# Order of loads and weight preparation in the opening of an mLSTM and MLP kernel

## The chip, the core and the metric

The kernel runs on one core of a Trainium2 chip. The metric is the device time of one execution in microseconds. TensorE is called PE here, VectorE DVE, ScalarE ACT, GpSimd POOL and the engine that issues most DMAs SP, as in the profile.

## The reference

The reference has two parts. The first is a recurrence over 768 positions, for 4 batches of 8 heads with head size 40. The second is a multilayer perceptron on its output, 3072 tokens by 320, with a hidden width of 2048:

```
m_new = max(f + m, i);  fs = exp(f + m - m_new);  is = exp(i - m_new)
C = fs * C + is * outer(v, k);   n = fs * n + is * k
y = sigmoid(o) * (C @ q) / max(|n . q|, 1)
x = y as tokens by 320;   h = x @ w_in;   out = (h * sigmoid(h)) @ w_out
```

The inputs are float32, but w_in and w_out arrive as 64-bit floats.

## The kernel before

**Units.** The recurrence is done in chunks of 128 positions. A unit is one chunk of one batch with all 8 heads, so there are 24 units, and units 0 to 3 are the first chunk of the four batches. For each unit the kernel loads `raw` (q and k, transposed), `D` (the running sum of the log forget gates, spread over all partitions) and `kvo` (k, v and the output gate). Then it goes through these steps:

- `decay` (L346): POOL masks D, ACT takes eight exponentials per unit (L364).
- `scores` (L374): PE multiplies k and q (L393), DVE weighs v (L405) and the scores (L412).
- `values` (L416): PE multiplies scores and v (L432), DVE divides and applies the gate and leaves `x` (L439 to L449).
- `state` (L455): PE makes the new state (L461), DVE masks it into `Cm` (L483).
- `xpose` (L490): PE transposes x (L494 to L497), ACT copies it into `xh` (L501) and DVE writes the rest into `xl` (L502). This feeds the perceptron.

**Steps.** Three units make a step of 384 tokens, eight steps in all. A step needs the x of its three units. It runs over 16 chunks of the hidden width: `mm1` (L517, products at L531) multiplies x with a chunk of w_in, ACT and DVE apply the activation, and `mm2` (L555, products at L571) multiplies the result with a chunk of w_out, two chunks later. Step 0 keeps the activation whole (g, L539), later steps split it in two.

**Weights.** The weights come in 18 parts, in the order c0, i0, o0, i1, o1, i2, o2, i3, o3, c4, i4 and so on. A part i holds rows 0 to 255 of w_in for two chunks of the hidden width, a part c holds rows 256 to 319 for eight chunks, and a part o holds the w_out rows of two chunks. `wload(n)` issues the DMAs of the next n parts (L166; L170 and L171 for c). `wmake(n)` makes the next n parts (L173): ACT takes the absolute value (L183), DVE turns the 64-bit float into a 32-bit one in four instructions (L184, L185, L188, L194), and for a part i or c ACT and DVE split it into two (L204 and L205, or L214 and L215). After each make, `wmake` loads one more part.

**What sets the order.** SP's order is that of the program, by hand. For the other engines a planner orders the instructions when the kernel is built: an earlier place in the program is a higher priority, and what is ready in its own reckoning goes first. DVE's order inside the first call of `gates` is by hand too. `gates(lo, hi)` (L101) works out the gate sums for some positions and writes them to DRAM (L124), where the loads of D read them. Raw tiles, weight parts and the x of a step share a pool of ten buffers (`NBIG`); the gates use four of these at the start. A load waits until a buffer is free.

The opening, L635 to L678, is a list of calls ahead of the loop over the steps. In the loop, `FILL` gives the number of weight parts that are made after each chunk of step 0.

Of the kernel before, what the change touches and what calls it, by code (L numbers as in the profile page):

```python
# [43 lines left out]
def mlstm_mlp_kernel(  # L44
# [56 lines left out]
    def gates(lo, hi):  # L101

        init = NEG if lo == 0 else m_t[:, lo - 1 : lo]
        nc.vector.tensor_tensor_scan(
            m_t[:, lo:hi], f_t[:, lo:hi], i_t[:, lo:hi], init, op0=ALU.add, op1=ALU.max
        )

        l1 = max(lo, 1)
        eng = nc.vector
        eng.tensor_tensor(  # L110
            out=f_t[:, l1:hi], in0=f_t[:, l1:hi], in1=m_t[:, l1 - 1 : hi - 1], op=ALU.add
        )
        eng.tensor_tensor(
            out=f_t[:, l1:hi], in0=f_t[:, l1:hi], in1=m_t[:, l1:hi], op=ALU.subtract
        )
        nc.vector.tensor_scalar(f_t[:, l1:hi], f_t[:, l1:hi], -120.0, None, op0=ALU.max)
        if lo == 0:
            nc.vector.memset(f_t[:, 0:1], 0.0)
        for c in range(lo // L, hi // L):
            sl = slice(c * L, (c + 1) * L)  # L120
            nc.vector.tensor_tensor_scan(
                LF[:, sl], one.broadcast_to([BH, L]), f_t[:, sl], 0.0, op0=ALU.mult, op1=ALU.add
            )
        nc.sync.dma_start(LFd[:, 0:H, lo:hi], LF[:, lo:hi])  # L124
        nc.scalar.dma_start(LFd[:, H, lo:hi], LF[0:B, lo:hi])
        eng.tensor_tensor(
            out=i_t[:, lo:hi], in0=i_t[:, lo:hi], in1=m_t[:, lo:hi], op=ALU.subtract
        )
        eng.tensor_tensor(
            out=i_t[:, lo:hi], in0=i_t[:, lo:hi], in1=LF[:, lo:hi], op=ALU.subtract  # L130
        )
        c0, c1 = lo // L, hi // L
        pt = psA.tile([128, 512], F32, tag="a", name=f"pt{lo}")
        for c in range(c0, c1):
            nc.tensor.transpose(
                pt[:, c * BH : (c + 1) * BH], i_t[:, c * L : (c + 1) * L], ident[:BH, :BH]
            )
        nc.vector.tensor_copy(
            aT[:, c0:c1, :], pt[:, c0 * BH : c1 * BH].rearrange("p (c h) -> p c h", h=BH)
        )  # L140
# [105 lines left out]
    def wload(n):  # L246
        for p in parts[nload[0] : nload[0] + n]:
            p.load()
        nload[0] = min(nload[0] + n, len(parts))

    def wmake(n):

        for p in parts[nmade[0] : nmade[0] + n]:
            p.make()
            wload(1)
        nmade[0] = min(nmade[0] + n, len(parts))
# [335 lines left out]
    units = [Unit(n) for n in range(NU)]  # L592
    steps = {}

    def prep(n, k):
        if n >= NU:
            return
        u = units[n]
        if k == 0:
            u.split(0, 0)  # L600
            u.split(0, 1)
        elif k == 1:
            u.decay(0)
        elif k == 2:
            u.split(1, 0)
            u.split(1, 1)
        elif k == 3:
            u.decay(1)
        elif k == 4:
            u.misc()  # L610

    def prepare(n):
        for k in range(5):
            prep(n, k)
# [26 lines left out]
    prepare(0)  # L641
    units[1].load_qk()
    units[1].load_d()
    units[1].load_kvo()
    wload(1)
    units[2].load_qk()
    units[2].load_d()
    units[2].load_kvo()
    units[0].scores()
    prepare(1)  # L650
    gates(L, S)
    wload(2)
    units[1].scores()
    units[0].values()
    wmake(1)
    prepare(2)
    steps[0] = Step(0)
    units[0].xpose(steps[0])
    units[0].state()
    units[2].scores()  # L660
    units[1].values()
    units[1].xpose(steps[0])
    wmake(1)
    units[1].state()
    units[2].values()
    units[2].xpose(steps[0])
    units[2].state()
    wmake(1)
    units[3].load_d()
    units[3].load_qk()  # L670
    units[3].load_kvo()
    wmake(2)
    units[4].load_d()
    prepare(3)
    units[4].load_qk()
    wmake(1)
    units[4].load_kvo()
# [91 lines left out]
```

## Time and profile before

| | us |
|---|---|
| median of 3 runs | 524.79 |
| lowest and highest | 523.82, 524.89 |
| the profiled execution | 527.61 |
| its span | 525.8 |

| engine | busy in the span, us |
|---|---|
| PE | 487.5 |
| DVE | 334.8 |
| ACT | 268.4 |
| POOL | 95.0 |

The profile is of one execution. A row of its timeline gives the start in us, the duration in us, the engine, the line of the kernel, the operation, what is written and read, and the shapes; in brackets stands how long the engine had been idle and what ended that. SPq rows are DMA issues, not the transfers. A row of the view by stretches gives the busy time of each engine in a stretch, with the count of instructions, the granted clock, the share of time that the 16 DMA engines were busy, and the bytes that they moved.

### The profile page before, as it was taken

What the parts mean: (1) busy time and instruction counts of PE and PEld (TensorE: products, weight loads), DVE (VectorE), ACT (ScalarE), POOL (GpSimd) and SP (SyncE); (2) the same over time, 40 slices, a digit from 0 to 9 for tenths busy, and PEclk for the clock granted to TensorE, in tenths of its full rate; (3) what the DMA queues carried; (4) which work ended last, traced back from release to release, by engine and by line L of the source; (5) the groups of instructions that cost most, each with busy time, mean ns of one, the idle gap of its engine ahead of it and who ended that gap; (6) DMA issues with size and microseconds to landing.
All of it is one profiled execution on the core that took longest, in us unless ns stands there. A gap on an engine that the chain in (4) does not pass through costs nothing.

```text
span 525.8 us, 8615 instructions
## 1 busy us (share of the span) xinstructions
PE 487.5 (93%) x3098; PEld 466.6 (89%) x3098; DVE 334.8 (64%) x687; ACT 268.4 (51%) x647; POOL 95.0 (18%) x139
## 2 busy tenths in 40 slices
PE   1498899999979989999999999999999999999996
PEld 1496888888969989998999899998998999999996
DVE  6399999853678768576755866439565644444342
ACT  1546775632666647476556464446464433334332
POOL 0111223422134324122402210221210000000000
PEclk9999999999999989999999999999999999999999
DMA  3999896153476496646614634233571001001001
GB/s 112 264 345 239 238 327 183 58 153 106 134 161 181 107 226 168 175 110 161 175 47 107 175 87 140 73 107 104 149 193 31 28 1 39 0 1 39 1 2 37
DMA packets 52525, 65.54 MB, mean 125 GB/s; under 512 B 3195, under 2 KB 40479, under 8 KB 52483
## 3 DMA queue, kind: packets, MB, share of 16 engines
q1 hardware_dynamic: 48963, 60.95, 42.4%
q10 hardware_dynamic: 3520, 4.04, 2.2%
q8 instruction: 24, 0.39, 0.3%
q14 instruction: 18, 0.15, 0.1%
HBM read 60.94 MB, written 4.04 MB: 124 GB/s over the span
## 4 chain that ended last, share of the span: by engine, by line
PE 58%; DMA 22%; ACT 9%; DVE 7%; issue 2%; POOL 1%; SPq 1%; POOLq 0%; ACTq 0%; DVEq 0%
PE pout L571 23%; PE ph L531 23%; DMA D<-LFd 11%; PE po L432 5%; DMA raw<-in_qk_dram 5%; ACT D L364 4%; DMA kvo<-in_kvo_dram 3%; DVE st L339 3%; PE ps L393 3%; ACT st L337 2%; PE po L423 1%; ACT gh L549 1%; DMA wro<-in_w_out_dram 1%; DVE th L544 1%; PE pu L461 1%
## 5 line engine op out<-in xcount | busy, mean ns | idle before, releaser
L531 PE MATMUL ph<-xh,wh 128*128 128x384 f32 x384 | 136.5, 355 | 6.5 <-DVE th L544 4.7
L531 PE MATMUL ph<-xl,wh 128*128 128x384 f32 x384 | 131.2, 342 | 0.0
L571 PE MATMUL pout<-woh,gh 128*128 128x320 f32 x336 | 107.3, 321 | 3.7 <-ACT gh L549 3.3
L544 DVE SCALAR_TENSOR_TENSOR th<-th,ph 128x384 f32<-128x384 f32 x112 | 61.3, 549 | 75.7 <-ACT th L535 75.5
L571 PE MATMUL pout<-wol,gh 128*128 128x320 f32 x336 | 103.0, 308 | 0.0
L550 DVE TENSOR_TENSOR gl<-th,gh 128x384 fp32r<-128x384 f32 x112 | 65.7, 589 | 55.6 <-ACT gh L549 53.5
L571 PE MATMUL pout<-woh,gl 128*128 128x320 f32 x336 | 99.8, 311 | 1.4 <-DVE gl L550 1.3
L535 ACT ACTIVATE th<-ph 128x384 f32<-128x384 f32 x128 | 62.0, 485 | 65.4 <-PE ph L531 62.4
L531 PE MATMUL ph<-xh,wl 128*128 128x384 f32 x256 | 87.7, 342 | 0.0
L531 PEld LDWEIGHTS ph<-xh,wh 128*128 128x128 f32 x384 | 73.3, 191 | 9.3 <-DVE th L544 5.9
L549 ACT CAST gh<-th 128x384 fp32r<-128x384 f32 x112 | 57.0, 510 | 47.4 <-DVE th L544 45.2
L531 PEld LDWEIGHTS ph<-xl,wh 128*128 128x128 f32 x384 | 73.3, 191 | 0.9
L364 ACT ACTIVATE D<-D,aT 128x128 f32<-128x128 f32 x192 | 59.8, 389 | 16.7 <-POOL D L354 16.4
L571 PEld LDWEIGHTS pout<-woh,gh 128*128 128x128 f32 x336 | 63.2, 188 | 5.4 <-ACT gh L549 4.7
L571 PEld LDWEIGHTS pout<-woh,gl 128*128 128x128 f32 x336 | 61.7, 188 | 2.7 <-DVE gl L550 2.7
L571 PEld LDWEIGHTS pout<-wol,gh 128*128 128x128 f32 x336 | 63.2, 188 | 0.1
L432 PE MATMUL po<-kvo,D 128*128 128x41 f32 x384 | 54.2, 299 | 0.5 <-issue 0.4
L432 PEld LDWEIGHTS po<-kvo,D 128*128 128x128 f32 x384 | 53.3, 215 | 1.4 <-ACT wti L183 0.8
L339 DVE TENSOR_TENSOR st<-raw,st 40x512 fp32r<-40x512 f32 x64 | 45.6, 713 | 11.6 <-ACT st L337 10.0
L354 POOL TENSOR_SCALAR_AFFINE_SELECT D<-D 128x512 f32<-128x512 f32 x48 | 33.0, 711 | 89.6 <-ACT fd L351 63.8
L531 PEld LDWEIGHTS ph<-xh,wl 128*128 128x128 f32 x256 | 48.8, 191 | 0.0
L337 ACT CAST st<-raw 120x512 fp32r<-120x512 f32 x64 | 35.6, 619 | 17.7 <-DMA raw<-in_qk_dram 17.7
(77 smaller groups left out, 548.4 us busy)
## 6 DMA issues: line engine op xcount, KB each, us to landing
raw<-in_qk_dram SPq DMA_DIRECT2D x32, 480.0 KB
D<-LFd SPq DMA_DIRECT2D x24, 512.0 KB
kvo<-in_kvo_dram SPq DMA_DIRECT2D x24, 484.0 KB
wro<-in_w_out_dram SPq DMA_DIRECT2D x8, 640.0 KB
wri<-in_w_in_dram SPq DMA_DIRECT2D x8, 512.0 KB
out_dram<-ob ACTq DMA_DIRECT2D x24, 160.0 KB
qt<-in_qp_dram SPq DMA_DIRECT2D x20, 180.0 KB
lq<-LFd SPq DMA_DIRECT2D x60, 60.0 KB
```

The lines of the kernel that those rows point to most:

```text
L337: nc.scalar.copy(t, raw)
L339: nc.vector.tensor_tensor(out=t[r0 : r0 + D, :], in0=raw[r0 : r0 + D, :], in1=t[r0 : r0 + D, :].bitcast(F32), op=ALU.subtract,)
L354: nc.gpsimd.affine_select(out=d, in_=d, compare_op=ALU.is_ge, fill=NEG, base=0, pattern=[[0, HH], [1, L]], channel_multiplier=-1,)
L364: nc.scalar.activation(d[:, h, :], d[:, h, :], AF.Exp, bias=aT[:, c, r + h : r + h + 1])
L393: nc.tensor.matmul(ps[:, j, :], k_[:, cs], q_[:, cs], start=True, stop=True)
L432: nc.tensor.matmul(po[:, h, :], self.Dm[:, h, :], self.vt[:, h, :], start=first, stop=(h == H - 1))
L531: nc.tensor.matmul(ph, w, x, start=(i == 0), stop=(i == len(ops) - 1))
L535: nc.scalar.activation(th, ph, AF.Tanh, scale=0.5)
L544: nc.vector.scalar_tensor_tensor(out=th, in0=th, scalar=1.0, in1=ph, op0=ALU.add, op1=ALU.mult)
L549: nc.scalar.copy(gh, th)
L550: nc.vector.tensor_tensor(out=gl, in0=th, in1=gh.bitcast(F32), op=ALU.subtract)
L571: nc.tensor.matmul(self.po[t], g[:, ts], w, start=(fc == 0 and i == 0), stop=(last and i == len(ops) - 1),)
```

## The change

The change reorders the calls of the opening. No computation is added or removed.

- The load of i0 goes ahead of the load of kvo of unit 1, and the loads of o0 and i1 follow directly, ahead of everything of unit 2.
- Unit 2's three loads are spread: raw behind unit 1's preparation, D behind the second call of `gates` (and so behind its write), kvo behind unit 1's scores.
- One more part (i2) is loaded right after c0 is made.
- i0 is made after unit 0's state, o0 after unit 2's scores, both ahead of unit 1's values; i1 after unit 3's loads.
- Unit 2's values go ahead of unit 1's transposes, its state behind the loads of D and raw of unit 3, and its transposes behind unit 3's preparation.
- One part fewer is made ahead of the loop, five instead of six. The number of parts loaded ahead of the loop stays ten.

```diff
     prepare(0)
     units[1].load_qk()
     units[1].load_d()
+    wload(1)
     units[1].load_kvo()
-    wload(1)
-    units[2].load_qk()
-    units[2].load_d()
-    units[2].load_kvo()
+    wload(2)
     units[0].scores()
     prepare(1)
+    units[2].load_qk()
     gates(L, S)
-    wload(2)
+    units[2].load_d()
     units[1].scores()
+    units[2].load_kvo()
     units[0].values()
     wmake(1)
+    wload(1)
     prepare(2)
     steps[0] = Step(0)
     units[0].xpose(steps[0])
     units[0].state()
+    wmake(1)
     units[2].scores()
+    wmake(1)
     units[1].values()
+    units[2].values()
     units[1].xpose(steps[0])
-    wmake(1)
     units[1].state()
-    units[2].values()
-    units[2].xpose(steps[0])
-    units[2].state()
-    wmake(1)
     units[3].load_d()
     units[3].load_qk()
+    units[2].state()
     units[3].load_kvo()
-    wmake(2)
+    wmake(1)
     units[4].load_d()
     prepare(3)
+    units[2].xpose(steps[0])
     units[4].load_qk()
     wmake(1)
     units[4].load_kvo()
```

## The prediction

> **What bounds the kernel now.** I read the page first: the share of each engine and the forty slices.
>
> ```profile
> PE 487.5 (93%) x3098; PEld 466.6 (89%) x3098; DVE 334.8 (64%) x687; ACT 268.4 (51%) x647; POOL 95.0 (18%) x139
> PE   1498899999979989999999999999999999999996
> DVE  6399999853678768576755866439565644444342
> ```
>
> PE is the bound over the span, and it is full from about the fifth slice (13 us each) on. What PE loses, it loses in the first five slices, and there DVE shows 9 from the third to the seventh. The change touches only this opening, so the next view is the busy time by stretches (columns: us, then busy us and instruction count of PE, PEld, DVE, ACT and POOL, then granted clock, DMA share and GB/s).
>
> ```profile
> 16.00:26.00 10.00, 4.86 (x20) 4.37 (x21) 2.14 (x5) 5.65 (x20) 2.46 (x4) 1.00 1.05 283
> 26.00:36.00 10.00, 10.00 (x55) 9.40 (x54) 8.64 (x21) 5.90 (x16) 1.67 (x2) 1.00 1.04 367
> 36.00:46.00 10.00, 8.07 (x36) 6.87 (x35) 10.00 (x27) 4.33 (x8) 0.39 (x1) 1.00 0.98 282
> 65.00:110.00 45.00, 44.11 (x249) 37.06 (x248) 40.29 (x77) 26.48 (x65) 14.97 (x17) 1.00 0.64 196
> ```
>
> From 16 to 46 us the DMA engines are full (shares 1.05, 1.04, 0.98). DVE is nearly idle until 26 (2.14 of 10) and full afterwards. From 65 us PE is full (44.11 of 45), so whatever is won or lost in the moment at which the step's first products start running stays until the end.
>
> What DVE does in its full stretch is seen by asking the same view for 26.1 to 53.5 us: first all instructions, then those that touch the work tiles of the w_in parts (wti), then those of the w_out parts (wto).
>
> ```profile
> 26.10:53.50 27.40, 25.04 (x119) 21.92 (x120) 26.14 (x61) 15.68 (x37) 3.34 (x4) 1.00 1.00 287
> ```
>
> ```profile
> 26.10:53.50 27.40, 9.40 (x16) 4.15 (x7) 1.00 1.00 287
> ```
>
> ```profile
> 26.10:53.50 27.40, 7.95 (x12) 3.17 (x4) 1.00 1.00 287
> ```
>
> Of 26.14 us of DVE, 9.40 + 7.95 = 17.35 us make weights. A w_in part is five DVE instructions, so 9.40 x 5/16 = 2.94 us; a w_out part four, 7.95 x 4/12 = 2.65 us. The first two chunks of the first matrix product need of these only part i0.
>
> The timeline of DVE shows both ends of that stretch.
>
> ```profile
> 22.44 1.29 DVE L412 TENSOR_TENSOR D<-ps,D 128x512 f32<-128x512 f32 x2
> 26.12 0.50 DVE L405 TENSOR_TENSOR vw<-kvo,D 128x328 f32<-128x328 f32 x1 [2.40 <-ACT D L364]
> 26.62 0.43 DVE L184 TENSOR_SCALAR wti<-wti 128x512 f32<-128x512 f32 x1
> 32.74 0.50 DVE L405 TENSOR_TENSOR vw<-kvo,D 128x328 f32<-128x328 f32 x1 [1.13 <-issue]
> 36.27 0.68 DVE L412 TENSOR_TENSOR D<-ps,D 128x512 f32<-128x512 f32 x1
> 53.44 0.55 DVE L502 TENSOR_TENSOR xl<-px,xh 128x384 fp32r<-128x384 f32 x1
> ```
>
> The first instruction of i0 (L184) runs at 26.62, just after DVE has stood 2.40 us. The last input of the first product is xl of unit 2, done at 53.44 + 0.55 = 53.99, although unit 2's scores were weighed by 36.95. On PE:
>
> ```profile
> 11.37 2.08 PE L393 MATMUL ps<-raw 40*128 40x128 f32 x16
> ...
> 54.60 1.85 PE L432 MATMUL po<-kvo,D 128*128 128x41 f32 x8
> 56.25 0.67 PE L531 MATMUL ph<-xl,wh 128*128 128x384 f32 x1
> 56.71 0.52 PE L531 MATMUL ph<-xh,wl 128*128 128x384 f32 x1
> 57.03 0.52 PE L531 MATMUL ph<-xh,wh 128*128 128x384 f32 x1
> ...
> 62.96 0.44 PE L531 MATMUL ph<-xh,wh 128*128 128x384 f32 x1 [1.69 <-DVE g L539]
> 63.24 0.34 PE L531 MATMUL ph<-xl,wh 128*128 128x384 f32 x1
> 63.41 0.34 PE L531 MATMUL ph<-xh,wl 128*128 128x384 f32 x1
> ```
>
> The dense products start at 56.25, behind xl and the rest of unit 3's values (54.60), then stand once for 1.69 us at 62.96 because DVE is behind with the first g. So the opening is bound by DVE's backlog, and the backlog begins at 26 us.
>
> **The order of loads.** SP issues in program order, and this part of it is what the change rewrites:
>
> ```profile
> 14.38 1.95 SPq L301 DMA_DIRECT2D kvo<-in_kvo_dram  x1
> 16.37 0.43 SPq L166 DMA_DIRECT2D wri<-in_w_in_dram  x1
> 16.84 1.87 SPq L290 DMA_DIRECT2D raw<-in_qk_dram  x2
> 19.27 0.39 SPq L278 DMA_DIRECT2D D<-LFd  x1
> 20.45 1.72 SPq L301 DMA_DIRECT2D kvo<-in_kvo_dram  x1
> 22.27 0.63 SPq L124 DMA_DIRECT2D LFd<-LF  x1
> 22.94 0.44 SPq L166 DMA_DIRECT2D wro<-in_w_out_dram  x1
> 23.42 0.47 SPq L166 DMA_DIRECT2D wri<-in_w_in_dram  x1
> ```
>
> ```profile
> wro<-in_w_out_dram SPq DMA_DIRECT2D x8, 640.0 KB
> wri<-in_w_in_dram SPq DMA_DIRECT2D x8, 512.0 KB
> ```
>
> These are kvo of unit 1, i0, unit 2's three loads, the second write of LF, o0 and i1. Who waits for them is seen on ACT:
>
> ```profile
> 23.23 0.47 ACT L369 ACTIVATE kvo<-kvo 128x320 f32<-128x320 f32 x1 [1.05 <-DMA kvo<-in_kvo_dram]
> 23.60 2.43 ACT L364 ACTIVATE D<-D,aT 128x128 f32<-128x128 f32 x8
> 25.94 0.65 ACT L183 ACTIVATE wti<-wri 128x512 f32<-128x512 f32 x1
> 28.89 0.22 ACT L351 ACTIVATE fd<-D 120x8 f32<-120x8 f32 x1 [2.30 <-DMA D<-LFd]
> ```
>
> kvo of unit 1, issued at 14.38, came 8.85 us later; D of unit 2, issued at 19.27, came 9.62 us later. The queue is deep, so what is put ahead in it pushes back the rest by its bytes. I take 325 GB/s, the mean of the first two stretches (283 and 367).
>
> **i0 ahead of kvo of unit 1.** i0 takes the place at 14.38 and lands about 23.3. ACT's first step on it (0.65) ends at about 24.0, and DVE can start i0 at 24.0 instead of 26.62; DVE was free from 22.44 + 1.29 = 23.73 to 26.12. That fills 2.1 us. If the planner leaves ACT's step behind unit 1's exponentials (2.43 from 23.60), the gain is nil; at best it is the 2.40. I take 2.1, because ACT itself stood 1.05 us just before 23.23. kvo of unit 1 comes 512 KB or 1.6 us later, at 24.8; its DVE user ran at 26.12, held by the exponentials, so this costs nothing, and 0.65 on them is covered by i0 on DVE.
>
> **o0 and i1 ahead of unit 2.** They now come before unit 2's three loads instead of after them, and so can fill the second hole of DVE, 1.13 us at 32.74: from 0 to 1.13, and I take 0.5, because part of this hole is issue time. In exchange unit 2's loads come 1152 KB or 3.6 us later: D at 32.5 instead of 28.89, its weighed scores at 40.6 instead of 36.95 at worst. I cost this at nothing, because between 24 and 37 us DVE has i0 (2.94), o0 (2.65), i1 (2.94) and the vw and two weighings of unit 1 and the values of units 0 and 1, all of which it did after 26 in the old order. If that cover is gone, the price is 3.6 us.
>
> **The rest of SP's queue.** Unit 2's raw tile is now the eleventh in a pool of ten; it takes that of unit 0, whose scores end at 11.37 + 2.08 = 13.45, long before its turn. D of unit 2 goes behind the second write of LF, but reads only columns that the first wrote; no wait is added. i2 and i3 are issued ahead of unit 3's loads, where in the old order i3 came behind them: unit 3 comes 1.6 us later. Its values (54.60) stand in PE's order ahead of the dense products, so this costs 0 to 1.6 us; I take 0, since by the sum DVE reaches unit 3 earlier.
>
> **The makes.** The number of weight makes ahead of the loop falls from six to five: i2 (2.94 us of DVE) goes behind the first chunk. In the old order it was nearly finished ahead of xl of unit 2, so this is worth 0 to 2.94 at xl. I take 0: DVE's order fills every wait of unit 2's chain with whatever weights have landed, and they land earlier now. Unit 2's transposes go behind the make of i1 and unit 3's exponentials on ACT (2.43 plus 0.47 of the gate): 0 to 2.9 us lost. I take 0, since i1 is done long before and unit 3's D comes before xh. State of units 1 and 2 and the values change places within DVE work that all has to be done: nothing.
>
> **Sum.** 2.1 + 0.5 = 2.6 us less. The profiled execution took 527.61 us (span 525.8, 1.8 around it); it becomes 525.0. The median of the runs shown, 524.79, lies 2.82 us below the profiled one, so I say 522.2.
>
> One rule could change this term. The starts of the dense products are 0.32 us apart at 56.71 and 0.17 at 63.24, while the granted clock column reads 1.00 in every stretch and PE had been busy 10.00 of 10.00 us from 26 to 36 without becoming faster. The slow stretch thus follows the dense products, and in the sum it moves with them, unchanged.
>
> The Trainium skill, "TensorE: Matmul & The Clock Gate", Part 1, says that the array runs at half clock until a busy window of about 3.4 us has passed, and that this window runs freely, not from the kernel's start. By that rule the slow stretch could end up to one window sooner or later than it now does, an estimate from the page of 3.4 x (1 - 0.17/0.32) = 1.6 us either way, so 520.6 to 523.8 in place of 522.2. The full stretch from 26 to 36 us, which should have ended the slow clock by the same rule, speaks against taking it as it stands.
>
> **Rivals.**
> Nothing measurable: the planner puts i0 behind the exponentials, or the 2.6 us are spent in later weight parts ahead of xl (there were 17.35 us of them). For it: DVE's order has always put landed weights first. Against: work done earlier on a full engine is not lost, and the 1.69 us at 62.96 is DVE's lateness too. Time 524.8.
>
> Slower: unit 2 sets the start. Its loads come 3.6 us later and its chain to xl, 53.99 - 28.89 = 25.1 us in the old trace, keeps its length because the same weights are put between its links. The first dense product comes 3.6 us later; the 1.69 us stall goes, since DVE is ahead by then: 1.9 us more, 526.7. It decides if DVE stands for more than 1 us between 30 and 45 us, or if xl of unit 2 ends after 54. For it: the transposes are also put back. Against: DVE was full from 36 to 46, so data was not what it waited for.
>
> Much faster: the freed order lets unit 2's chain go ahead of two more weight parts (i2 and o2, 2.94 + 2.65 = 5.6 us) that ran ahead of xl though the first four chunks don't need them. Then 2.6 + 5.6 = 8.2 less, 516.6. Against: DVE is at 40.29 of 45 us until 110, so what is put off must soon be done.
>
> **How the numbers follow.** Forecast 0.47, its own range 519.8 to 523.7 (a gain of 1.05 us, below which it is nothing, up to 2.40 + 1.13 and half of i2's 2.94, 5.0 us); much faster 0.10; nothing 0.17; slower 0.26. So faster by over 0.2% (about what a measurement of this kernel can tell from no change, 1.05 us) 0.57, within 0.17, slower 0.26. The range runs from 518.0, which leaves out most of much faster, to 527.0, which holds the slower case at its price of 526.7 and a little of unit 3's 1.6 us; slower with both (528.3) is left out, and with it some 0.18 in all.
>
> **What would show it.** Right: L184 on i0 near 24 us; DVE about 4 of 10 us busy from 16 to 26 and without holes until 60; ACT's fd of unit 2 near 32.5; xl of unit 2 done by about 51.5; first dense product near 53.5; no stall of 1.7 us on g. Wrong: DVE holes of more than 1 us from 30 to 45 us, xl after 54, or PE below 44 of 45 us from 65 to 110, which would mean that DVE no longer keeps up.

## The result

The changed kernel is slower: 529.63 us (median of 5 runs) against 523.83 for the kernel before, a ratio of 1.0131 with a 95% interval of 1.0093 to 1.0168. The prediction said 522.2, with a range up to 527.0. Ratios, here and below, are estimated from executions in the faster of the chip's two states alone, so they need not equal the quotient of two medians (1.0111 here). The profiled execution of the changed kernel took 534.57 us, 6.96 more than the profiled one of before, and its traces are compared below.

From the page of the changed kernel, the slices of PE and DVE:

```profile
PE   1488997999979989998999999999999999999996
DVE  6579999745568587665755767447574555444342
```

DVE is busier in the second slice (5, it was 3) and idler in the third (7, it was 9). PE's seventh slice, 80 to 93 us, is down to 7 from 9. The stretches that the prediction quoted, for the changed kernel:

```profile
16.00:26.00 10.00, 4.19 (x18) 3.66 (x17) 4.11 (x8) 5.49 (x19) 2.72 (x4) 1.00 1.03 316
26.00:36.00 10.00, 10.00 (x55) 9.70 (x55) 8.53 (x20) 3.30 (x8) 2.97 (x2) 1.00 1.07 332
36.00:46.00 10.00, 7.07 (x32) 6.20 (x33) 7.30 (x18) 6.64 (x16) 0.25 (x1) 1.00 1.03 290
65.00:110.00 45.00, 41.24 (x227) 34.16 (x227) 38.40 (x68) 24.32 (x59) 11.88 (x14) 0.96 0.55 165
```

DVE gained 1.97 us of work before 26 (4.11 against 2.14) and lost 2.70 from 36 to 46 (7.30 against 10.00). PE's own loss is in the last row: it is busy 41.24 of 45 us where it had 44.11. The timeline of the changed kernel shows the start of it:

```profile
24.36 0.42 DVE L184 TENSOR_SCALAR wti<-wti 128x512 f32<-128x512 f32 x1
...
32.75 0.22 ACT L351 ACTIVATE fd<-D 120x8 f32<-120x8 f32 x1 [3.79 <-DMA D<-LFd]
33.03 3.21 POOL L354 TENSOR_SCALAR_AFFINE_SELECT D<-D 128x512 f32<-128x512 f32 x2 [8.84 <-ACT fd L351]
...
38.59 0.50 DVE L405 TENSOR_TENSOR vw<-kvo,D 128x328 f32<-128x328 f32 x1 [3.42 <-issue]
...
56.00 0.54 DVE L502 TENSOR_TENSOR xl<-px,xh 128x384 fp32r<-128x384 f32 x1
...
57.01 1.43 PE L461 MATMUL pu<-vw,kvo 128*120 128x123 f32 x6
...
59.88 0.67 PE L531 MATMUL ph<-xl,wh 128*128 128x384 f32 x1
```

i0 starts 2.26 us earlier on DVE (24.36 against 26.62). Unit 2's D is there 3.86 later (32.75 against 28.89), and DVE then has a hole of 3.42 us. xl of unit 2 ends at 56.54, which is 2.55 later; PE first runs a state product (57.01) and the rest of unit 3's values, and the products with xl start 3.63 later than the 56.25 of before. (One product, with xh alone, runs ahead of xl in both, at 54.97 here and at 53.05 before.)

A second loss follows 30 us on. The same view, at the eighth and ninth chunk and at the first product of step 1:

```profile
85.39 0.58 PE L531 MATMUL ph<-xh,wh 128*128 128x384 f32 x1
...
87.03 1.78 PE L571 MATMUL pout<-wo,g 128*128 128x320 f32 x6
...
88.09 0.47 ACT L535 ACTIVATE th<-ph 128x384 f32<-128x384 f32 x1
88.27 1.22 POOL L372 TENSOR_TENSOR qt<-qt,lq 120x384 f32<-120x384 f32 x1 [0.72 <-ACT lq L371]
88.56 1.48 DVE L188 SCALAR_TENSOR_TENSOR wti<-wri,wti 128x512 uint32<-128x512 uint32 x1
...
90.80 1.24 DVE L225 TENSOR_TENSOR wol<-wo,woh 128x640 fp32r<-128x640 f32 x1
91.97 0.54 DVE L539 SCALAR_TENSOR_TENSOR g<-th,ph 128x384 f32<-128x384 f32 x1
92.56 0.44 PE L531 MATMUL ph<-xh,wh 128*128 128x384 f32 x1 [3.76 <-DVE g L539]
...
94.28 3.25 PE L571 MATMUL pout<-wo,g 128*128 128x320 f32 x6
...
126.06 0.58 PE L531 MATMUL ph<-xh,wh 128*128 128x384 f32 x1
```

and in the kernel before:

```profile
82.93 0.58 PE L531 MATMUL ph<-xh,wh 128*128 128x384 f32 x1
...
86.55 0.58 PE L531 MATMUL ph<-xh,wh 128*128 128x384 f32 x1
...
120.08 0.58 PE L531 MATMUL ph<-xh,wh 128*128 128x384 f32 x1
```

At the eighth chunk the changed kernel is only 2.46 us late (85.39 against 82.93). Then PE waits 3.76 us for a g that stands on DVE behind other work, weights above all (L188, L225): its th is there at 88.56, and DVE begins it at 91.97. The ninth chunk starts at 92.56 against 86.55, 6.01 late, and step 1 at 126.06 against 120.08, 5.98 late. So most of the 6.96 us is there by the end of step 0. The stall has a second price, seen in the granted clock (the column behind the five engines) of the changed kernel:

```profile
90.00:95.00 5.00, 2.44 (x10) 2.24 (x11) 5.00 (x11) 3.61 (x12) 2.23 (x3) 0.88 0.27 77
95.00:100.00 5.00, 5.00 (x27) 3.53 (x26) 3.97 (x7) 1.96 (x4) 0.00 (x0) 0.78 0.00 0
```

The clock falls to 0.88 and 0.78 behind the stall, and six products of mm2 take 3.25 us (94.28) where they take 1.78 at 87.03. The Trainium skill, "TensorE: Matmul & The Clock Gate", HAM oscillation, says that idle gaps of PE over about 3.4 us bring the slow clock back; the gap of 3.76 us agrees with that.

### The profile page after: what moved, and what is told of

It reads as the page before. It is cut to its first block, busy times and chain, and to the rows that moved or that the text cites. A ratio compares the mean times of both kernels' runs of the same rounds, so it can differ in the third digit from the quotient of the medians.

```text
span 532.8 us, 8614 instructions
## 1 busy us (share of the span) xinstructions
PE 490.2 (92%) x3098; PEld 469.0 (88%) x3098; DVE 332.8 (62%) x687; ACT 268.6 (50%) x647; POOL 94.8 (18%) x139
## 4 chain that ended last, share of the span: by engine, by line
PE 60%; DMA 21%; DVE 8%; ACT 6%; SPq 2%; issue 2%; POOL 1%; POOLq 0%; ACTq 0%; DVEq 0%
PE ph L531 25%; PE pout L571 24%; DMA D<-LFd 11%; PE po L432 5%; DMA raw<-in_qk_dram 4%; DMA wrc<-in_w_in_dram 3%; ACT D L364 3%; PE ps L393 2%; DVE st L339 2%; DMA lq<-LFd 2%; PE po L423 2%; PE pu L461 1%; POOL D L354 1%; DVE th L544 1%; SPq L290 1%
## 5 line engine op out<-in xcount | busy, mean ns | idle before, releaser
L550 DVE TENSOR_TENSOR gl<-th,gh 128x384 fp32r<-128x384 f32 x112 | 65.2, 585 | 55.9 <-ACT gh L549 52.0
L354 POOL TENSOR_SCALAR_AFFINE_SELECT D<-D 128x512 f32<-128x512 f32 x48 | 36.0, 773 | 90.2 <-ACT fd L351 68.5
```

The costliest lines, as they stand in the source:

```text
L354: nc.gpsimd.affine_select(out=d, in_=d, compare_op=ALU.is_ge, fill=NEG, base=0, pattern=[[0, HH], [1, L]], channel_multiplier=-1,)
L550: nc.vector.tensor_tensor(out=gl, in0=th, in1=gh.bitcast(F32), op=ALU.subtract)
```

## Experiments

Every kernel was run beside the kernel before on the same chip. The last two columns are from one trace of each. The first counts the weight parts that DVE finishes (L194) ahead of xl of unit 2; the kernel before has 7 and the changed one 8. The second is the start of PE's first product with xl, 56.25 us before and 59.88 changed. (The traced execution of e12 took 523.59 us, well above its median of 518.03.)

| run | what | ratio | 95% | parts ahead | xl product |
|---|---|---|---|---|---|
| e12 | before, o0 and i1 loaded later | 0.9886 | 0.9848–0.9925 | 4 | 51.35 |
| e18 | changed, o0, i1, i2 loaded later | 0.9922 | 0.9890–0.9954 | 4 | 48.32 |
| e16 | before, i0 first, o0 and i1 later | 0.9949 | 0.9916–0.9982 | 5 | 51.84 |
| e6 | new loads, old steps (as e1) | 0.9919 | 0.9875–0.9964 | 6 | 52.89 |
| e1 | new loads, old steps | 0.9923 | 0.9881–0.9965 | 6 | 53.21 |
| e10 | before, unit 2's values early | 0.9985 | 0.9939–1.0030 | 6 | 52.45 |
| e14 | e1 with five makes | 1.0008 | 0.9963–1.0052 | 6 | 50.43 |
| e11 | before, unit 3's loads later | 1.0019 | 0.9980–1.0059 | 6 | 53.38 |
| e17 | changed, no early load of i2 | 0.9994 | 0.9958–1.0030 | 7 | 57.59 |
| e3 | before, i0 first | 1.0010 | 0.9972–1.0048 | 7 | 56.66 |
| e4 | changed, o0 and i1 loaded behind unit 2 | 1.0019 | 0.9976–1.0063 | 7 | 58.13 |
| e8 | changed, makes of i0 and o0 back | 1.0037 | 0.9984–1.0091 | 7 | 59.24 |
| e7 | changed, six makes, no early load | 1.0051 | 1.0000–1.0103 | 7 | 57.69 |
| e9 | changed, unit 2's values back | 1.0021 | 0.9988–1.0054 | 8 | 55.62 |
| e15 | before, early load of i2, five makes | 1.0097 | 1.0063–1.0131 | 8 | 59.91 |
| e13 | e1 with the early load of i2 | 1.0112 | 1.0055–1.0168 | 8 | 51.65 |
| e2 | new steps, old loads | 1.0117 | 1.0077–1.0156 | 8 | 57.99 |
| e5 | changed, transposes back (as changed) | 1.0119 | 1.0039–1.0199 | 8 | 59.59 |

**Loads or steps.** The first theory (A in the expectations) was the slower rival of the prediction, to which two signs of the profile point, the hole of 3.42 us and xl after 54: unit 2's data comes too late. The rival theory put the loss in the steps and makes. e1 is the kernel before with the new order of loads alone:

```diff
+    wload(1)
     units[1].load_kvo()
-    wload(1)
-    units[2].load_qk()
-    units[2].load_d()
-    units[2].load_kvo()
+    wload(2)
...
+    units[2].load_qk()
     gates(L, S)
-    wload(2)
+    units[2].load_d()
     units[1].scores()
+    units[2].load_kvo()
```

> The order of loads alone: i0 ahead of kvo of unit 1, o0 and i1 ahead of unit 2, unit 2's loads spread; steps and makes as before (six makes, ten parts loaded). Theory A (unit 2's data come 3.6 us later and DVE runs dry for some 3 us at 35 us): most of the loss is here, 2.5 to 5 us above the kernel before, with a DVE hole of over 2 us between 33 and 40 us. Theory B (the loss comes from the new order of steps and from five makes instead of six): within 1 us of the kernel before, or up to 2.6 us below it.

e2 is the changed kernel with these lines undone, and so has all the rest, the early load of i2 too.

> The order of steps and makes alone (five makes, one extra load of i2), loads of i0, o0, i1 and of unit 2 as before. Theory A: within 1.5 us of the kernel before, no hole in DVE after 26 us other than the old one of 1.1 us. Theory B: 4 to 6 us above the kernel before, with PE standing over 3 us on a g in step 0 between 80 and 100 us, as in the changed kernel (3.76 us).

e1 is faster, 0.9923, and e2 slower, 1.0117, as the rival theory had it; but the stall of over 3 us that it named is not in e2's trace, where PE stands 2.06 us at 65.2 and 1.34 at 91.6. The timeline of e1 has the same late data:

```profile
33.54 0.22 ACT L351 ACTIVATE fd<-D 120x8 f32<-120x8 f32 x1 [3.66 <-DMA D<-LFd]
...
39.24 0.50 DVE L405 TENSOR_TENSOR vw<-kvo,D 128x328 f32<-128x328 f32 x1 [3.44 <-issue]
...
51.12 0.54 DVE L502 TENSOR_TENSOR xl<-px,xh 128x384 fp32r<-128x384 f32 x1
...
53.21 0.52 PE L531 MATMUL ph<-xl,wh 128*128 128x384 f32 x1
```

The data is even later (33.54) and the hole as long (3.44), yet xl ends at 51.66 and the products with xl start at 53.21, some 3 us ahead of before. So late data alone does not make the loss, although its signs were there; e15 below has the loss without late data.

**Single loads.** e3 is the kernel before with i0 moved alone:

```diff
+    wload(1)
     units[1].load_kvo()
-    wload(1)
     units[2].load_qk()
```

> The kernel before with one swap: i0 loaded ahead of kvo of unit 1. Unit 2's loads stay where they were. Theory A, with the gain forecast for DVE: 0 to 2.1 us below the kernel before, L184 on i0 near 24.4 us, fd of unit 2 still near 28.9 us. Theory B says the same for the loads, and sees no loss since steps and makes are as before: the two differ in nothing here, it prices the gain alone.

e4 is the changed kernel with o0 and i1 loaded behind unit 2:

```diff
     units[1].load_kvo()
-    wload(2)
...
     units[2].load_kvo()
+    wload(2)
```

> The changed kernel with o0 and i1 loaded behind unit 2's three loads again; all else as changed. Theory A: 3 to 5 us below the changed kernel, so within 2.5 us of the kernel before; fd of unit 2 near 29 us, first dense product before 57 us. Theory B: stays 4 to 6 us above the kernel before, with a PE stall of over 3 us on a g between 80 and 100 us.

e11 is the kernel before with two makes, and with them the loads of i3 and o3, ahead of unit 3's loads:

```diff
+    wmake(2)
     units[3].load_d()
     units[3].load_qk()
     units[3].load_kvo()
-    wmake(2)
```

> The kernel before with unit 3's three loads moved behind those of i3 and o3, 1152 KB or some 3.6 us later; nothing else. As built, six L194 stand ahead of xl of unit 2, and unit 3's values stand behind the first dense products, as with the loads alone. Theory C1: 3 to 5 us below the kernel before, although no load of i0, o0, i1 or unit 2 has moved. Theory C2: 2 to 4 us below. If the loads alone won through an earlier i0 (the gain that was forecast): no gain.

e3 gives 1.0010: the 2.1 us of DVE that the forecast counted on are filled and are worth nothing. e4 gives 1.0019, as the theory of late data had it: with o0 and i1 behind unit 2 no loss can be measured. But e4 also has one part fewer ahead of xl, and its ten runs scatter, from 522.14 to 533.97 us with a median of 528.29, so its figure is among the least sure here. e11 gives 1.0019, no difference.

**Single steps.** e5 is the changed kernel with the transposes of unit 2 earlier, e6 is e1 with the same transposes later:

```diff
# e5
     units[3].load_qk()
+    units[2].xpose(steps[0])
     units[2].state()
...
     prepare(3)
-    units[2].xpose(steps[0])
```

```diff
# e6
     units[2].values()
-    units[2].xpose(steps[0])
     units[2].state()
...
     prepare(3)
+    units[2].xpose(steps[0])
```

> The changed kernel with unit 2's transposes back ahead of its state; all else as changed. The loads alone were faster and the steps alone slower, so the loss lies in the steps. Theory B1 (the place of unit 2's transposes: they come late in PE's and DVE's order, behind unit 3's scores and behind more weight parts): 5 to 9 us below the changed kernel, so at or below the kernel before; xl of unit 2 before 53 us, PE makes unit 2's transposes ahead of unit 3's scores. Theory B2 (the early makes of i0 and o0 and one make fewer): within 2 us of the changed kernel.

> The kernel with the new order of loads alone, and unit 2's transposes put behind unit 3's preparation, as the change does. Theory B1: 5 to 9 us above the loads alone, with unit 3's values ahead of the dense products in PE's order and xl of unit 2 after 54 us. Theory B2: within 2 us of the loads alone.

e7 is the changed kernel with six makes, and without the early load:

```diff
     wmake(1)
-    wload(1)
     prepare(2)
...
     units[3].load_kvo()
-    wmake(1)
+    wmake(2)
```

> The changed kernel with six makes ahead of the loop again (i1 and o1 together, then i2) and without the extra load, so that ten parts are loaded as before. Theory B1: within 2 us of the changed kernel. Theory B2 (i2 in the loop and the fill of step 0 one part late): 3 to 6 us below the changed kernel, without the PE stall of 3.8 us on a g at 92 us.

e8 is the changed kernel with the makes of i0 and o0 in later places:

```diff
     units[0].state()
-    wmake(1)
     units[2].scores()
-    wmake(1)
...
     units[1].xpose(steps[0])
+    wmake(1)
     units[1].state()
...
     units[2].state()
+    wmake(1)
     units[3].load_kvo()
```

> The changed kernel with the makes of i0 and o0 in their old places (behind unit 1's transposes, behind unit 2's state). Theory B1: within 2 us of the changed kernel. Theory B2: 3 to 6 us below it, since unit 1's and 2's chains on DVE go ahead of weights again.

e9 is the changed kernel with unit 2's values behind unit 1's state, and e10 the kernel before with them ahead of it:

```diff
# e9
     units[1].values()
-    units[2].values()
     units[1].xpose(steps[0])
     units[1].state()
+    units[2].values()
```

```diff
# e10
     units[1].values()
+    units[2].values()
     units[1].xpose(steps[0])
     wmake(1)
     units[1].state()
-    units[2].values()
```

> The changed kernel with unit 2's values back behind unit 1's state; the early load of i2 stays. In the order of instructions as built, eight L194 (one a weight part) stand on DVE ahead of xl of unit 2, as in the changed kernel (before: seven, loads alone: six), but unit 3's values stand behind the first dense products on PE, as with the loads alone (before and changed: ahead). Theory C1 (what costs is unit 3's values and state, 4.9 us at the slow rate, ahead of the dense products): 3 to 5 us below the kernel before. Theory C2 (what costs is weight parts on DVE ahead of xl, 2.8 us each): 1 to 4 us above the kernel before.

> The kernel before with one step moved: unit 2's values directly behind unit 1's, as the change has it; loads and makes as before. As built, six L194 stand ahead of xl of unit 2 (before: seven), and unit 3's values still stand ahead of the dense products. Theory C1: within 1.5 us of the kernel before. Theory C2: 2 to 4 us below it. If this place of the values is bad in itself: 4 to 7 us above it.

e5 and e6 turned out to have the same instructions in the same order on every engine as the changed kernel and as e1: the planner does not care where these transposes stand. Their ratios, 1.0119 and 0.9919, say how well a ratio repeats (1.0131 and 0.9923). As e5 is the changed kernel run once more, its trace shows what in the first one belongs to the kernel. Two views of e5, the timeline and the stretches:

```profile
59.59 0.67 PE L531 MATMUL ph<-xl,wh 128*128 128x384 f32 x1
...
66.06 0.69 PE L494 MATMUL px<-ident,x 128*128 128x128 f32 x2 [2.27 <-DVE x L449]
...
124.89 0.58 PE L531 MATMUL ph<-xh,wh 128*128 128x384 f32 x1
```

```profile
65.00:70.00 5.00, 3.94 (x20) 3.00 (x21) 4.87 (x9) 3.68 (x11) 1.91 (x2) 0.59 0.94 218
70.00:75.00 5.00, 5.00 (x18) 4.02 (x18) 4.84 (x8) 3.21 (x8) 1.16 (x1) 0.73 1.05 348
```

The late start is there again (59.59, 3.34 behind the kernel before). The stall of 3.76 us at 92.56 is not; in its place PE waits 2.27 us for x at 66.06, and the slow clock follows there (0.59 and 0.73). Step 1 starts at 124.89, 4.81 late. So the late start belongs to the kernel, and where DVE then falls behind changes from one execution to the next; e5's profiled execution took 528.90 us, close to the median, so the 534.57 of the first holds a stall that is longer than usual.

By their ratios e8 and e9 each give back most of the loss (1.0037, 1.0021), and e10 shows that the early values alone cost nothing (0.9985). e8 scatters as e4 does, from 520.86 to 534.93 us, and the interval of e7 (1.0000 to 1.0103) holds anything from no loss to most of it. So none of these steps was seen to cost by itself.

The expectations of e9 to e12 weigh two theories: C1, that unit 3's values and state cost because they stand ahead of the dense products, and C2, that weight parts ahead of xl cost, 2.8 us each. Neither holds as it stands. C2's number came in e9 (1.1 us above before) and, at the edge, in e12 (6.0 below); C1's came in e10 (0.8 us below, although one part fewer stands ahead of xl); and e11 gained nothing, where both forecast a gain.

**What the load and the makes cost.** Of the kernels so far, all that are slower by 1% (the changed one, e2, e5) have the early load of i2 and one make fewer, which were tried apart and together (D1 is the theory that the early load costs, D2 that the missing make does). e13 adds the load to e1, e14 takes the make from e1, e15 does both to the kernel before:

```diff
# e13 and e15
     wmake(1)
+    wload(1)
     prepare(2)
```

```diff
# e14 and e15
     units[3].load_kvo()
-    wmake(2)
+    wmake(1)
```

> The new order of loads alone, plus the early load of i2 (each later part is then loaded one place earlier, i3 ahead of unit 3); six makes as before. As built, eight L194 stand ahead of xl of unit 2 (loads alone: six). Theory D1 (the early load is what costs: it hands DVE one more part and pushes unit 3 back): 4 to 6 us above the loads alone, so 0 to 2 us above the kernel before. Theory D2 (one make fewer costs): as the loads alone, 3 to 5 us below the kernel before.

> The new order of loads alone with five makes ahead of the loop in place of six and no early load of i2 (nine parts loaded ahead of the loop). As built, six L194 stand ahead of xl of unit 2. Theory D1: as the loads alone, 3 to 5 us below the kernel before. Theory D2: 0 to 2 us above the kernel before.

> The kernel before with the early load of i2 and five makes, nothing else: that half of the change to the makes without the new order of loads and of steps. As built, eight L194 stand ahead of xl of unit 2 (before: seven). If this pair costs by itself: 3 to 6 us above the kernel before, as the steps and makes together did (1.0117). If it costs only beside the new order of loads: within 1.5 us.

The early load takes e1 from 0.9923 to 1.0112; one make fewer, without it, only to 1.0008. Neither theory has both numbers right: e13 is more than the 0 to 2 us above before that D1 gave it, and e14 is slower than e1 with the same six parts ahead of xl, as D2 had it. So one make fewer, taken from e1, seems to cost too, and the count does not see it. e15 has the old load order, and none of the change's moves but these two; which of them costs there it does not say. Its timeline has unit 2's D as early as before (29.14 against 28.89), and still the late start:

```profile
29.14 0.22 ACT L351 ACTIVATE fd<-D 120x8 f32<-120x8 f32 x1 [2.26 <-DMA D<-LFd]
...
55.78 0.54 DVE L502 TENSOR_TENSOR xl<-px,xh 128x384 fp32r<-128x384 f32 x1
...
59.91 0.67 PE L531 MATMUL ph<-xl,wh 128*128 128x384 f32 x1
```

59.91 against 59.88 in the changed kernel. Late data without the loss (e1), and the loss without late data (e15): what they differ in, among other things, is how much weight work DVE does ahead of xl. The view by stretches, for L194 alone (one for each part), up to the start of that xl, first before, then changed, e15 and e1; the count of instructions in brackets is what matters:

```profile
0.00:53.44 53.44, 5.48 (x7) 1.00 0.85 239
```

```profile
0.00:56.00 56.00, 5.78 (x8) 1.00 0.84 236
```

```profile
0.00:55.78 55.78, 6.60 (x8) 1.00 0.86 245
```

```profile
0.00:51.12 51.12, 4.30 (x6) 1.00 0.84 240
```

e13 shows that the loss can also come later. Its xl is early (51.05 + 0.55), its first product with xl starts at 51.65, but the stall on g comes at the ninth chunk, and the clock falls for most of 10 us. Two views of e13, the timeline and the stretches:

```profile
51.05 0.55 DVE L502 TENSOR_TENSOR xl<-px,xh 128x384 fp32r<-128x384 f32 x1
...
87.33 0.44 PE L494 MATMUL px<-ident,x 128*128 128x128 f32 x2 [1.03 <-DVE x L449]
...
90.39 0.69 PE L531 MATMUL ph<-xh,wh 128*128 128x384 f32 x1 [1.07 <-DVE g L539]
```

```profile
90.00:95.00 5.00, 4.61 (x16) 4.18 (x16) 5.00 (x10) 1.49 (x4) 3.88 (x4) 0.50 0.57 192
95.00:100.00 5.00, 5.00 (x13) 3.60 (x13) 3.68 (x7) 4.32 (x12) 0.00 (x0) 0.51 0.00 0
```

The clock is 0.50 and 0.51 (of 1.00) there, behind two idle gaps of only 1.03 and 1.07 us.

**Loading weights later.** If weights ahead of unit 2's chain cost, loading them later must gain. e12 moves o0 and i1 in the kernel before, and e16 does the same in e3:

```diff
     gates(L, S)
-    wload(2)
...
     units[2].scores()
+    wload(2)
     units[1].values()
```

> The kernel before with o0 and i1 loaded later, just ahead of unit 1's values, so that fewer weight parts are there to be made: as built, four L194 stand ahead of xl of unit 2, and unit 3's scores and values stand behind the first dense products. Theory C1: 3 to 5 us below the kernel before. Theory C2: 6 to 9 us below. If the forecast was right that weights made early are worth their time: 3 us or more above, since DVE has more left to do in step 0.

> The kernel before with i0 loaded ahead of kvo of unit 1 and o0 and i1 later, just ahead of unit 1's values: the two ends that the runs point to, i0 early for DVE's idle time and no spare weight part in unit 2's way. As built, five L194 stand ahead of xl of unit 2. If the two add: 6 to 9 us below the kernel before. If the number of parts ahead of xl alone sets the time: between the loads alone (six, 0.9923) and o0 and i1 late (four, 0.9886), 4 to 6 us below.

e17 takes only the early load of i2 out of the changed kernel:

```diff
     wmake(1)
-    wload(1)
     prepare(2)
```

> The changed kernel without its early load of i2; all else stays. In DVE's order as built only 4 weight parts then stand ahead of xl of unit 2, where the changed kernel has 8. If the number of parts ahead of xl sets the time (now our main theory), this lands with the other kernel that has 4 (0.9886): 0.985 to 0.995 of the kernel before, 516 to 521 us, with the first dense product near 51 us. If the one make fewer or the other moves of the steps cost of themselves (the rival), about half of the change's loss stays: 1.003 to 1.01, 526 to 529 us.

e18 keeps all ten loads of the changed kernel, three of them later:

```diff
     units[1].load_kvo()
-    wload(2)
...
     wmake(1)
-    wload(1)
     prepare(2)
...
+    wload(3)
     units[1].values()
```

> The changed kernel with the loads of o0, i1 and i2 all just ahead of unit 1's values; ten parts are still loaded ahead of the loop, and makes and steps stay. 4 weight parts stand ahead of xl of unit 2. If what counts is when weights land, and not how many loads there are, this is as fast as the kernel without the early load: 0.985 to 0.995. If the tenth part loaded costs by its bytes on the DMA queues or by the buffer that it holds, it stays near the changed kernel: 1.005 to 1.015.

e12 is the fastest kernel of the study: 518.03 us against 524.58, 0.9886, from moving one line of the kernel before. e16 gives 0.9949, 2.7 us below, which is short of both forecasts, and with five parts it is no faster than e1 with six. e18 gives 0.9922: with every step and make of the change in place, and as many parts loaded, later loads turn 1.0131 into 0.9922. That speaks against a cost of the tenth load by its bytes; it holds its buffer for a shorter time here, so a cost by the buffer is not excluded. Stretches of e18 and e17, counted as above:

```profile
0.00:47.72 47.72, 2.85 (x4) 1.00 0.85 251
```

```profile
0.00:53.79 53.79, 5.11 (x7) 1.00 0.85 241
```

For e17 the expectation gave four parts, and the trace shows seven: the count on which it rested was wrong. At 0.9994 it lies among the other kernels with seven, and the loss of the change is gone with that one line. Neither theory's number there came true: it is not as fast as e12, and no half of the loss stayed. Its xl starts at 53.79, 2.21 us ahead of the changed kernel's 56.00, for one part less. Step 1 gains more than that:

```profile
57.59 0.67 PE L531 MATMUL ph<-xl,wh 128*128 128x384 f32 x1
...
119.03 0.58 PE L531 MATMUL ph<-xh,wh 128*128 128x384 f32 x1
```

Against it the changed kernel, as run in e5, is 2.00 us late at the first product with xl (59.59) and 5.86 late at step 1 (124.89). So the later start is about a third of what is lost by step 1; the rest is lost inside step 0, where PE stalls on DVE and the clock falls.

e18 also shows that an early start is not all. It starts its products with xl 7.9 us before the kernel before, and gives all of it back by step 1, at first because DVE is not ready with g:

```profile
48.32 0.69 PE L531 MATMUL ph<-xl,wh 128*128 128x384 f32 x1 [0.70 <-DVE xl L502]
...
57.62 0.69 PE L531 MATMUL ph<-xh,wh 128*128 128x384 f32 x1 [2.70 <-DVE g L539]
...
121.44 0.67 PE L531 MATMUL ph<-xh,wh 128*128 128x384 f32 x2 [1.06 <-ACT xh L501]
```

Its step 1 starts at 121.44, even later than the 120.08 of before, with one chunk of mm2 more done by then. So in this execution e18 wins its time behind that point, and no run shows by what.

**What stays open.** The count orders the kernels roughly: six parts go from 0.9919 to 1.0019, and e9 with eight gives 1.0021. The start of the products with xl orders them worse: e10 starts 3.80 us ahead of before and is no faster, e13 starts 4.60 ahead and is 1.1% slower, e17 and e4 start 1.34 and 1.88 behind and lose nothing that can be measured. e4, e8 and e9 have the early load and no clear loss. What is shown is that the early load of i2 decides in the changed kernel (e17) and beside the new order of loads (e13), and that three loads put later undo the loss (e18). That it acts through unit 2's chain is argued from the count; the rest may lie in the order that the planner builds on DVE for the whole of step 0, which was not taken apart.

## Why the prediction was wrong

**i0 ahead of kvo of unit 1.** The times were right: i0 at 24.36 (24.0 forecast), DVE busy 4.11 of 10 from 16 to 26. The worth was wrong. 2.1 us were to come off the end; alone (e3) they gave 1.0010. In e3 xl of unit 2 ends at 53.73, only 0.26 earlier than before, so the time gained on DVE did not reach it. Filling an idle stretch of a loaded engine helps only if what it does is next on the path.

**o0 and i1 ahead of unit 2.** The shift was right: D at 32.75, 32.5 forecast. That it costs nothing was argued from DVE having enough to do, and this cover did not hold: the hole of 1.13 us became one of 3.42 in place of closing by 0.5. But by itself this costs nothing: e1 has the same hole and is faster than before.

**The makes.** This is the step that failed. "DVE's order fills every wait of unit 2's chain with whatever weights have landed, and they land earlier now" was true, and was booked as zero, with nothing below it. The same habit of DVE's order has a price: parts that land earlier are also put ahead of unit 2's chain, and one part is about 2.8 us of DVE by the prediction's own rows (2.94 and 2.65). In the changed kernel eight parts stand ahead of xl, not seven, although a make fewer stands ahead of the loop; xl is 2.55 later. The early load of i2 decides: without it 0.9994 (e17), with it 1.0131. The prediction priced that load only by what it pushes back (unit 3's loads, 0 to 1.6 us, taken as 0), not by the part that it hands DVE. One make fewer ahead of the loop, worth "0 to 2.94" by the text, had the other sign in e14 against e1, 1.0008 against 0.9923; in the changed kernel without the early load it was not seen to cost (five makes 0.9994 in e17, six makes 1.0051 in e7, with intervals that overlap).

**Transposes, unit 3, state and values.** Zero was right for the transposes (the same program, e5) and for unit 3's loads (e11). It was right for unit 2's values in the kernel before (e10) and wrong in the changed one: without them (e9) 1.0021, with them 1.0131. Costing each edit alone missed that.

**The start that stays.** The prediction took it that what is won or lost at the start of step 0's products stays until the end. This failed too. The changed kernel starts 3.63 us late, is 2.46 late at the eighth chunk and 6.01 at the ninth, behind one stall; and e10, which starts 3.80 us early, is no faster than before.

**The stall of 1.69 us on g.** The prediction took it as DVE's lateness, which an early start would shrink. It went from 62.96, but others took its place, 3.76 at 92.56 in one execution and 2.27 at 66.06 in another, with the slow clock behind them. The sign named for this, PE below 44 of 45 us from 65 to 110, came (41.24).

**The rivals.** The slower rival gave 526.7, and its two signs were in the profile; its mechanism, late data, is not enough for the loss (e1) and not needed for it (e15). That its time came nearest was luck. The much faster rival, at 0.10, had the lever that won most: letting unit 2's chain go ahead of more parts. e12 does that, four parts in place of seven, and gains 1.14%, 6.0 us of 524.58; only, the change moved the lever the other way. What spoke against it, that what is put off must soon be done, is what e18 shows in part.

## What to carry to other kernels

On an engine with a backlog, ask of each piece of work when it is next needed, not how early it can be done: an earlier load can be a loss when it lets work that is not yet needed go ahead of work that is. When a planner fills gaps with whatever has landed, the place of a load is a priority, and delaying a load can be the cheapest way of reordering an engine. Predicted signs may all come true with another cause, so find a kernel with the sign and without the loss, and one with the loss and without the sign. And an early start of the main products is worth little while the engine that feeds them is behind.

## What the hardware showed

A stall of PE can cost more than its length. The 3.76 us at 92.56 were followed by products at half rate, as were the 2.27 us at 66.06 in e5, and in e13 gaps of 1.03 and 1.07 us with small products between them were followed by two stretches of 5 us at a clock of 0.50 and 0.51; the gaps of e5 and e13 are under the 3.4 us of the Trainium skill's rule, so the rule does not cover them as it is worded. Nor does every gap of that size do it: in e9 PE stood 1.89 us at 90.53, and the clock stayed at 1.00 from 90 to 105.

Some work on POOL and DVE at the same time was slow. In the kernel before, POOL's mask of unit 0 took 1.22 us while DVE was idle; that of unit 2 took 1.67, and L194 on DVE, which began beside it, took 1.01:

```profile
18.70 1.22 POOL L354 TENSOR_SCALAR_AFFINE_SELECT D<-D 128x512 f32<-128x512 f32 x2 [17.39 <-ACT fd L351]
...
29.18 1.67 POOL L354 TENSOR_SCALAR_AFFINE_SELECT D<-D 128x512 f32<-128x512 f32 x2 [5.69 <-ACT fd L351]
29.34 1.01 DVE L194 SCALAR_TENSOR_TENSOR wti<-wri,wti 128x512 uint32<-128x512 uint32 x1
...
96.61 0.68 DVE L194 SCALAR_TENSOR_TENSOR wti<-wri,wti 128x512 uint32<-128x512 uint32 x1
```

L194 takes 0.68 at 96.61. In the changed kernel the mask of unit 2 took 3.21 (33.03), and L188 on DVE took 1.48 (88.56) while POOL ran L372 (88.27, 1.22 us); so a part of the stall of 3.76 us may come from there. The mask of unit 1 in the kernel before, beside L412, which reads one of its inputs from PSUM, took 1.24 (22.25) and was not slowed. The Trainium skill, "SBUF — State Buffer", Who interferes with whom, says that a DVE instruction with two inputs in SBUF contends with a GpSimd instruction that reads SBUF. The direction agrees; no run here took it apart.
